# More unsplit tiles, a port in the planner's costs, and the first batch's global queries moved beside tiles 16 to 31

## The chip, the cores and the metric

The kernel runs on one core of a Trainium2 chip. The metric is the device time of one execution in microseconds (us). A core has five engines that run their own instruction streams and meet at semaphores: TensorE (PE in the profile, with its weight loads as PEld), VectorE (DVE), ScalarE (ACT), GpSimd (POOL) and SyncE (SP), which here only issues DMAs. TensorE writes to PSUM; the other data lies in SBUF.

## The reference

Attention with two kinds of queries feeds an MLP with a maximum in it. There are 8 batches, 8 heads, 512 local and 32 global positions and 64 dimensions a head.

```python
k_all = concat([k_g, k_l]); v_all = concat([v_g, v_l])
out_g = softmax(scale * q_g @ k_all.T) @ v_all            # 32 global queries see everything
s_ll  = where(|i - j| <= 32, scale * q_l @ k_l.T, -1e9)   # local queries: a band, and the globals
s_l   = concat([scale * q_l @ k_g.T, s_ll])
out_l = softmax(s_l) @ concat([v_g, v_l])
x = concat([out_g, out_l], axis=2).transpose(0, 2, 1, 3).reshape(8 * 544, 512)
h = max(max(x @ w1, x @ w2), x @ w3)                      # 512 -> 768
return h @ w_out                                          # 768 -> 512
```

## The kernel before

**Tiles.** Two heads make a pair, so there are 4 pairs a batch and 32 in all. A pair's 512 local queries are cut into 4 tiles of 128, so there are 128 tiles; tile number = 4 * pair + t. `SEQ` is the order in which they are taken: the 16 tiles of the first batch first, then 16, 17 and on. Per tile, `scores` makes the banded scores for both heads (PE into PSUM tile `S`, a reducing DVE instruction at L325, the exponential on ACT at L327, a scaling by `times`), a DMA brings them to a buffer `prob`, `trans` transposes them on PE into PSUM tile `T` (L345, L346) and copies them to `pt`, and `pv` multiplies with the values into PSUM tile `O` (L384 or L392). Scores are made three tiles ahead.

**Split and unsplit.** In most tiles every operand is split into a rounded number and a remainder (tiles `qs`, `kst`, `vs`, the second half of `pt`): a copy makes the first, a subtraction the second, and PE multiplies with both. In the first tiles the operands are used whole in plain float32: `NATK` names the tiles whose queries and keys are unsplit, `NAT` the number of tiles whose probabilities and values are (both 20). An unsplit `pv` needs one copy out of `O`; a split one needs a copy and three additions (L398, L400).

**Global queries.** `glob` (two steps) and `glob_soft` make the 32 global queries' softmax of one pair, which six small DMAs bring to `probg`; `transg` transposes a quarter of it for each tile on PE (L364), into an `S` tile, and copies it beside the tile's own probabilities, so that `pv` treats both at once. `S` tiles have two PSUM buffers, `T` and `O` one each. The first batch's tiles go without: its global queries are made at the end by `late`, a pair after the other: loads, `glob`, `glob_soft`, three transposes (L490), 12 small products (L500).

**The MLP.** `moe_local(b)` yields after every matmul, and `fill(n)` puts n of its matmuls at a place in the attention: 432 matmuls with 256 columns (L424) and 72 with 512 (L445) for the first batch, which are spread over tiles 8 to 31 of `SEQ`; 216 and 72 with 512 columns for each other batch b, beside the attention of batch b + 1. After the last tile come the last batch's MLP with the four `late` pairs among its matmuls, and `moe_glob` for all global queries.

**Weights.** The 24 weight pieces arrive as 8-byte floats. `convert` makes float32 of them with one ACT and four DVE instructions (L160 to L166), then a copy and a subtraction. That happens at tiles 0 to 23.

**Who does what.** `sub` (L97), `copy` (L103, L105) and `times` (L111, L113, L115) may run on several engines. `least` picks the one whose running total in `load` plus its cost is lowest; `spend` books fixed work, `settle` lets totals lag no more than 4.5 us behind the highest at each tile. The order on each engine is then set by the framework's scheduler from the program's order.

## Time and profile before

| what | value |
|---|---|
| time before, median of 3 (lowest, highest) | 860.33 us (859.11, 861.3) |
| the profiled execution: its own time, its span | 859.92 us, 858.0 us |
| PE, PEld busy | 95%, 80% of the span |
| DVE, POOL, ACT busy | 74%, 61%, 59% |
| mean granted TensorE clock | 0.99 |

The page gives for each engine its busy time and for each group of instructions how many there are, the mean time of one, and what ended the idle time before them. Matmuls overlap, so the mean of one (its latency) is longer than the step from one to the next; steps are read from the chain of waits, which gives a start, a length and a name for each piece of the work that ended last. Busy shares are means over stages with different limits, so the table by stretches of time is read first.

### The profile page before, as it was taken

The page shows a single profiled execution, that of the slowest core. Times are in us where ns is not written, and L with a number is a line of the kernel's source. Part 1 is how long each engine was busy: PE and PEld are TensorE (multiplying, and loading weights), DVE is VectorE, ACT ScalarE, POOL GpSimd, SP SyncE. Part 2 cuts the span into 40 slices and gives each one's busy share as a digit, 9 for nine tenths or more (in the row PEclk, how much of TensorE's full clock was granted, in tenths as well). Part 3 has the DMA queues.
Part 4 walks back from the last instruction along what each step waited for, and adds up shares of the span by engine and source line. Part 5 has one row for each costly group of instructions (what it writes and reads, how often), then busy time and mean ns, then how long its engine had stood idle before and what let it go on. Part 6 is the DMA issues. An engine that isn't in the chain of part 4 may idle for free.

```text
span 858.0 us, 16764 instructions
## 1 busy us (share of the span) xinstructions
PE 813.2 (95%) x4736; PEld 683.5 (80%) x4736; DVE 631.0 (74%) x2182; ACT 505.8 (59%) x1430; POOL 526.4 (61%) x695
## 2 busy tenths in 40 slices
PE   6877777999999999999999999999999999999997
PEld 5556667888888888888888888788888888777796
DVE  6999788978888887878787888787887876322111
ACT  6666566766675767676666666676667665212111
POOL 4779878766677667766776667666686656101211
PEclk9999799999999999999999999999999999999999
DMA  9843533353334333443325333433344332221000
GB/s 315 278 151 120 165 120 102 112 161 105 112 111 131 119 96 105 129 137 98 95 91 160 107 111 111 141 114 96 101 132 134 93 102 90 75 72 29 28 25 25
DMA packets 99580, 98.72 MB, mean 115 GB/s; under 512 B 21152, under 2 KB 87968, under 8 KB 99488
## 3 DMA queue, kind: packets, MB, share of 16 engines
q1 hardware_dynamic: 99344, 97.43, 36.5%
q8 instruction: 38, 0.62, 0.3%
q14 instruction: 54, 0.44, 0.2%
q10 hardware_dynamic: 144, 0.23, 0.1%
HBM read 60.39 MB, written 8.91 MB: 81 GB/s over the span
## 4 chain that ended last, share of the span: by engine, by line
PE 82%; DVE 5%; DMA 5%; POOL 4%; issue 2%; ACT 1%; SPq 0%; DVEq 0%; POOLq 0%; ACTq 0%
PE pm L424 47%; PE pm L445 16%; PE O L392 7%; PE S L322 5%; PE T L345 2%; DMA raw<-w_in 2%; PE T L346 2%; PE S L274 1%; POOL h L97 1%; DMA qn<-q_in 1%; POOL xs L97 1%; PE S L364 1%; POOL w L97 1%; POOL early L115 1%; DMA vraw<-v_in 1%
## 5 line engine op out<-in xcount | busy, mean ns | idle before, releaser
L424 PE MATMUL pm<-xs,w 128*128 128x512 f32 (+1 forms) x2160 | 501.5, 370 | 5.3 <-POOL w L97 3.8
L424 PEld LDWEIGHTS pm<-xs,w 128*128 128x128 f32 x2160 | 349.5, 191 | 56.2 <-POOL w L97 4.2
L445 PE MATMUL pm<-w,h 128*128 128x512 f32 x612 | 160.3, 399 | 1.8 <-POOL h L97 1.8
L97 POOL TENSOR_TENSOR qs<-qraw,qs 128x256 fp32r<-128x256 f32 x108 | 83.2, 770 | 75.6 <-issue 42.2
L97 POOL TENSOR_TENSOR h<-m,h 128x512 fp32r<-128x512 f32 (+1 forms) x60 | 72.3, 1205 | 87.8 <-ACT h L105 87.8
L445 PEld LDWEIGHTS pm<-w,h 128*128 128x128 f32 x612 | 107.2, 188 | 22.6 <-POOL h L97 3.7
L115 POOL TENSOR_SCALAR s<-s,z 128x224 f32<-128x224 f32 (+1 forms) x212 | 97.0, 467 | 42.8 <-ACT lox L105 18.5
L327 ACT ACTIVATE s<-s,nm 128x192 f32<-128x192 f32 (+1 forms) x224 | 103.3, 462 | 25.4 <-DVE nm L325 19.9
L433 DVE TENSOR_TENSOR m<-pm,m 128x512 f32<-128x512 f32 (+1 forms) x120 | 72.9, 607 | 49.4 <-PE pm L424 47.1
L97 DVE TENSOR_TENSOR pt<-T,pt 128x512 fp32r<-128x512 f32 x108 | 74.5, 690 | 38.8 <-ACT pt L105 36.4
L325 DVE CUSTOM_DVE_ANT_0 s<-S,mask 128x192 f32<-128x192 f32 (+1 forms) x224 | 74.6, 370 | 12.7 <-PE S L322 6.4
L97 POOL TENSOR_TENSOR vs<-vraw,vs 128x256 fp32r<-128x256 f32 x107 | 80.3, 751 | 4.9 <-ACT vs L105 4.0
L105 ACT CAST pt<-T 128x512 fp32r<-128x512 f32 x89 | 52.0, 584 | 46.9 <-PE T L346 46.8
L392 PE MATMUL O<-pt,vs 128*128 128x320 f32 (+1 forms) x432 | 77.8, 302 | 0.1
L392 PEld LDWEIGHTS O<-pt,vs 128*128 128x128 f32 x432 | 70.0, 189 | 9.3 <-DVE pt L97 0.3
L97 POOL TENSOR_TENSOR kst<-kraw,kst 64x576 fp32r<-64x576 f32 x48 | 70.6, 1471 | 5.6 <-DVE nm L325 1.5
L322 PEld LDWEIGHTS S<-kst,qs 128*128 128x128 f32 x432 | 64.4, 192 | 11.1 <-DVE nmg L278 3.2
L400 DVE TENSOR_TENSOR xr<-O,lox 64x160 f32<-64x160 f32 x216 | 67.9, 314 | 2.8
L105 ACT CAST qs<-qraw 128x256 fp32r<-128x256 f32 x90 | 36.6, 406 | 56.6 <-PE S L322 39.5
L322 PE MATMUL S<-kst,qs 128*128 128x192 f32 (+1 forms) x432 | 66.0, 275 | 1.2 <-DVE nmg L278 1.2
L398 DVE TENSOR_TENSOR lox<-O,lox 64x320 f32<-64x320 f32 x108 | 51.6, 478 | 13.4 <-ACT lox L105 7.2
L105 ACT CAST h<-m 128x512 fp32r<-128x512 f32 (+1 forms) x59 | 32.9, 558 | 40.6 <-DVE m L433 40.5
(118 smaller groups left out, 1196.4 us busy)
## 6 DMA issues: line engine op xcount, KB each, us to landing
vraw<-v_in SPq DMA_DIRECT2D x132, 128.0 KB, 2.3
qraw<-q_in SPq DMA_DIRECT2D x108, 128.0 KB, 2.2
prob<-s SPq DMA_DIRECT2D x56, 224.0 KB, 2.4
raw<-w_in SPq DMA_DIRECT2D x24, 512.0 KB, 4.8
prob<-s SPq DMA_DIRECT2D x56, 192.0 KB, 2.3
kraw<-k_in SPq DMA_DIRECT2D x27, 320.0 KB, 3.2
out_dram<-o SPq DMA_DIRECT2D x32, 256.0 KB, 2.3
qn<-q_in SPq DMA_DIRECT2D x21, 128.0 KB, 3.8
```

The costliest lines, as they stand in the source:

```text
L97: (dve if least(c) == "d" else pool).tensor_tensor(out=out, in0=a, in1=b, op=ALU.subtract)
L105: act.copy(out=out, in_=a)
L115: pool.tensor_scalar(out=out, in0=a, scalar1=col, scalar2=1.0, op0=ALU.mult, op1=ALU.mult)
L322: pe.matmul(ph[j][:, 0:n], lhsT=qs[sl][:, a, 128 * j:128 * j + 128], rhs=kst[p][:, j, c0:c0 + n], start=(a == 0), stop=(a == 1))
L325: dve.tensor_tensor_reduce(out=s[:, j, 0:n], in0=ph[j][:, 0:n], in1=mask[:, (1, 0, 1, 0)[t], 32 * (t == 0):32 * (t == 0) + n], scale=-0.12 ...
L327: act.activation(out=s[:, j, 0:n], in_=s[:, j, 0:n], func=AF.Exp, bias=nm[:, j:j + 1], scale=-1.0, accum_out=z[:, j:j + 1])
L392: pe.matmul(o[:, j, 0:320].rearrange("p (a q) -> p a q", a=2)[:, :, 0:n], lhsT=vs[sl][:, 2 * j + c].rearrange("p a d -> p (a d)"), rhs=pt[ ...
L398: dve.tensor_tensor(out=lo, in0=o[0:64, :, 160:320], in1=lo, op=ALU.add)
L400: dve.tensor_tensor(out=xr[p][64 * j:64 * j + 64, t], in0=o[0:64, j, 0:160], in1=lo[:, j], op=ALU.add)
L424: pe.matmul(ps[:, 0:n], lhsT=weight(3 * f + i, w)[:, 128 * k:128 * k + 128], rhs=xs[k][:, a, c0:c0 + n], start=(q == 0), stop=(q == 11))
L433: dve.tensor_tensor(out=m[:, 0:n], in0=ps[:, 0:n], in1=m[:, 0:n], op=ALU.max)
L445: pe.matmul(ps, lhsT=hh[f][:, a, 128 * t:128 * t + 128], rhs=weight(18 + f, w), start=(q == 0), stop=(q == 17))
```

## The change

1. `NATK` goes from 20 to 28 tiles and `NAT` from 20 to 26: queries and keys of tiles 20 to 27 and probabilities and values of tiles 20 to 25 are no longer split.
2. The first batch's global queries are made at tiles 16 to 31, a pair in four tiles, one step a tile after that tile's `pv`. A pair's keys and its four value tiles are loaded into one tile `side`, which takes the place of `early` (free after the first 16 tiles). The softmax is made in it; six windows of 128 columns are transposed by PE straight from it into one `S` tile, and one DVE multiplication with a 0/1 mask `cover` copies them out and clears what a window has too much. The six DMAs a pair through `probg` are gone. The end of the program holds no attention any more.
3. `transg` of a tile stands at the tile's own start, just ahead of the next tile's `trans`; it stood in the middle of the tile before.
[...]
5. The keys of pairs 5 and 6 are no longer split, so their `split_k` falls away.

```diff
-NATK = range(0, 20)
+NATK = range(0, 28)
...
-    load = {"a": 0.0, "d": 0.0, "p": 0.0}
+    load = {"a": 0.0, "d": 0.0, "p": 0.0, "x": 0.0}
+    shared = [True]
...
     def least(costs):
-        e = min(costs, key=lambda e: load[e] + costs[e])
-        load[e] += costs[e]
-        return e
+        if not shared[0]:
+            costs = {es[0]: ns for es, ns in costs.items()}
+        es = min(costs, key=lambda es: max(load[e] for e in es) + costs[es])
+        spend(es, costs[es])
+        return es[0]
...
     def sub(out, a, b, psum=False):
-        n = width(out)
-        c = {"d": n * 1.04 + (160 if psum else 110)}
+        n, k = width(out), 0 if shared[0] else 45
+        c = {"d" if psum else "dx": n * 1.04 + 75 + k + (40 if k and psum else 0)}
         if not psum:
-            c["p"] = n * 2.32 + 130
+            c["px"] = n * 2.32 + 80 + k
...
     def times(out, a, col):
-        n = width(out)
-        e = least({"d": n * 0.52 + 125, "a": n * 0.833 + 185, "p": n * 1.27 + 150})
+        n, k = width(out), 0 if shared[0] else 1
+        e = least({"dx": n * 0.52 + 60 + 65 * k, "a": n * 0.833 + 190, "px": n * 1.27 + 170 - 20 * k})
...
-    NAT = 20
+    NAT = 26
...
     def late(p):
-        load_k(p)
-        for t in range(4):
-            load_v(4 * p + t, p * 4 + t)
+        k, v = side[:, 0:640], side[:, 640:1664].rearrange("p (t x) -> p t x", t=4)
+        nc.sync.dma_start(out=k, in_=kin[p])
+        nc.sync.dma_start(out=v, in_=vin[4 * p:4 * p + 4].rearrange("t p x -> p t x"))
         yield
-        for i in range(2):
-            glob(p, i)
+        s, nm, z = side[0:64, 0:NG], small.tile([64, 2], F32, name="nmg"), small.tile([64, 2], F32, name="zg")
+        for i, (c0, n) in enumerate(SEG):
+            ps = psS.tile([128, 512], F32, name="S")
+            pe.matmul(ps[0:64, 0:n], lhsT=k[:, KW:KW + 2 * SG], rhs=k[:, c0:c0 + n], start=True, stop=True)
+            dve.tensor_tensor_reduce(out=s[:, 384 * i:384 * i + n], in0=ps[0:64, 0:n], ...)
         yield
-        glob_soft(p)
+        soft(s, nm, z)
         yield
-        gt = att.tile([128, 3, 128], F32, name="gt", tag="pt")
-        for i in range(3):
-            g = psS.tile([128, 512], F32, name="S")
-            pe.transpose(g.bitcast(F32R)[:, 0:128], probg[p % 2][:, i], identr)
-            copy(gt[:, i], g[:, 0:128], True)
-        yield
+        g = psS.tile([128, 512], F32, name="S")
+        for x, (t, c, c0) in enumerate(PARTS):
+            pe.transpose(g[:, 64 * x:64 * x + 64], side[0:64, c0:c0 + 128], one[0:64, 0:64])
+        gt = att.tile([128, 6, 64], F32, name="gt", tag="lox", bufs=1)
+        dve.tensor_tensor(out=gt, in0=g[:, 0:384]..., in1=cover.to_broadcast([128, 6, 64]), op=ALU.mult)
         o = psO.tile([128, 2, 512], F32, name="O")
...
         settle(4500)
+        shared[0] = i < 26
...
+        if i >= EARLY:
+            transg(sl)
         trans(tile_at(i + 1))
...
-            if i == 14:
-                split_k(5)
-                load_k(6)
         elif t == 3:
             split_k(p + 2)
+            if p == NP:
+                load_k(6)
             load_k(p + 3)
         fill(5 if first else 4)
         pv(sl)
+        if EARLY <= i < 32:
+            if i == EARLY:
+                side = const.tile([128, 2048], F32, name="side", tag="early")
+            if i % 4 == 0:
+                lates = late(i // 4 - 4)
+            next(lates)
...
         fill(3)
-        if i + 1 >= EARLY:
-            transg(tile_at(i + 1))
         fill(7)
...
     mm[0] = moe_local(B - 1)
-    for p in range(NP):
-        for _ in late(p):
-            fill(10)
     fill(400)
```

Three places show what it does to the engines' order. The first is POOL in the first 16 tiles; `early` is the probabilities' buffer there, `w_...<-spare` a weight's remainder, `xs` an MLP input's. Before:

```order
L115 TENSOR_SCALAR early<-early,z 128x224 x2
L97 TENSOR_TENSOR w_436<-spare,w_436 128x512
L97 TENSOR_TENSOR xs<-xr,xs 128x256
L115 TENSOR_SCALAR early<-early,z 128x224 x2
L97 TENSOR_TENSOR w_483<-spare,w_483 128x512
L115 TENSOR_SCALAR early<-early,z 128x192 x2
L97 TENSOR_TENSOR w_493<-spare,w_493 128x512
L97 TENSOR_TENSOR xs<-xr,xs 128x256
L97 TENSOR_TENSOR w_537<-spare,w_537 128x512
```

Of the change, from the same place (the third to the sixth weights' remainders on POOL):

```order
L125 TENSOR_SCALAR early<-early,z 128x224 x2
L103 TENSOR_TENSOR w_349<-spare,w_349 128x512
L103 TENSOR_TENSOR w_437<-spare,w_437 128x512
L103 TENSOR_TENSOR w_544<-spare,w_544 128x512
L103 TENSOR_TENSOR w_614<-spare,w_614 128x512
L103 TENSOR_TENSOR h_563<-m,h_563 128x256
```

Up to the first 160-column `pv`, POOL issues 9 scalings of `early` instead of 30, 7 weight remainders instead of 15, 3 remainders of `xs` instead of 7, and no remainder of `kst` instead of 2. DVE gets 8 more weight remainders and 4 of `xs`, ACT 18 scalings instead of 1.

The second place is PE in a tile of the later batches, with `S<-identr,probg` the global queries' transpose, `T` the tile's transpose and `pm` the MLP. Before:

```order
L392 MATMUL O<-pt,vs 128x320 x4
L424 MATMUL pm<-xs,w_493 128x512 x3
L364 MATMUL S<-identr,probg_96 128x128
L424 MATMUL pm<-xs,w_493 128x512 x7
L345 MATMUL T<-identr,prob_94 128x128
```

Of the change:

```order
L409 MATMUL O<-pt,vs 128x320 x4
L441 MATMUL pm<-xs,w_494 128x512 x10
L381 MATMUL S<-identr,probg_96 128x128
L362 MATMUL T<-identr,prob_94 128x128
L363 MATMUL T<-identr,prob_94 96x128
```

The global transpose now stands against the tile's own, behind ten MLP matmuls in a row.

The third place is PE in the last batch's MLP. Before, each of the four pairs stands there like this:

```order
L270 MATMUL S<-kn 64x384
L270 MATMUL S<-kn 64x160
L424 MATMUL pm<-xs,w_493 128x512 x12
L424 MATMUL pm<-xs,w_537 128x512 x12
L424 MATMUL pm<-xs,w_607 128x512 x5
L490 MATMUL S<-identr,probg_96 128x128 x2
L424 MATMUL pm<-xs,w_607 128x512 x2
L500 MATMUL O<-gt,vn 64x32 x2
```

Of the change, the first pair's last step, at tile 19 (its two scores, L504, stand at tile 17):

```order
L441 MATMUL pm<-xs,w_396 128x256 x10
L513 MATMUL S<-one,side 128x64 x6
L401 MATMUL O<-pt,vraw 64x160 x4
L441 MATMUL pm<-xs,w_396 128x256 x2
L441 MATMUL pm<-xs,w_437 128x256 x6
L362 MATMUL T<-identr,prob_94 128x128
L519 MATMUL O<-gt,side 64x32 x12
```

In the last batch's MLP the change has MLP matmuls alone.

More of the change, by code (lines that the diff above doesn't have):

```diff
@@ L77, in width, with spend @@
         return n
-    def spend(e, ns):
-        load[e] += ns
+    def spend(es, ns):
+        for e in es:
+            load[e] += ns
     def least(costs):
-        e = min(costs, key=lambda e: load[e] + costs[e])
-        load[e] += costs[e]
-        return e
+        if not shared[0]:
[3 more added lines that the diff above has]
+        return es[0]
     def settle(ns):
@@ L92, in sub @@
     def sub(out, a, b, psum=False):
-        n = width(out)
-        c = {"d": n * 1.04 + (160 if psum else 110)}
+        n, k = width(out), 0 if shared[0] else 45
+        c = {"d" if psum else "dx": n * 1.04 + 75 + k + (40 if k and psum else 0)}
         if not psum:
-            c["p"] = n * 2.32 + 130
+            c["px"] = n * 2.32 + 80 + k
         (dve if least(c) == "d" else pool).tensor_tensor(out=out, in0=a, in1=b, op=ALU.subtract)
     def copy(out, a, psum=False):
-        n = width(out)
-        c = {"d": n * (1.04 if psum else 0.52) + (160 if psum else 150), "a": n * 0.833 + (150 if psum else 190)}
+        n, k = width(out), 0 if shared[0] else 75
+        c = {"a": n * 0.833 + (80 if psum else 110) + k}
+        if psum:
+            c["d"] = n * 1.04 + 80 + k
+        else:
+            c["dx"] = n * 0.52 + 75 + k
         if least(c) == "d":
@@ L107, in times @@
     def times(out, a, col):
-        n = width(out)
-        e = least({"d": n * 0.52 + 125, "a": n * 0.833 + 185, "p": n * 1.27 + 150})
+        n, k = width(out), 0 if shared[0] else 1
+        e = least({"dx": n * 0.52 + 60 + 65 * k, "a": n * 0.833 + 190, "px": n * 1.27 + 170 - 20 * k})
         if e == "d":
@@ L118, in body @@
     make_identity(nc, one)
-    early = const.tile([128, 4, 2, 256], F32, name="early")
+    early = const.tile([128, 4, 2, 256], F32, name="early", tag="early")
     identr = const.tile([128, 128], F32R, name="identr")
@@ L127, in body @@
     qgz = const.tile([128, 2, 160], F32R, name="qgz")
+    cover = const.tile([128, 6, 1], F32, name="cover")
     def clear():
+        pool.memset(cover, 1.0)
+        for x, a, n in ((1, 0, 32), (2, 96, 32), (3, 0, 64), (4, 0, 32), (5, 64, 64)):
+            pool.memset(cover[a:a + n, x], 0.0)
         for t in (*probg, qgz):
@@ L166, in convert @@
         dve.scalar_tensor_tensor(out=c, in0=r[:, :, 0], scalar=29, in1=c, op0=ALU.logical_shift_right, op1=ALU.bitwise_or)
-        spend("d", 1900)
+        spend("dx", 1900)
         yield
@@ L285, in glob_soft, with soft @@
         s, nm, z = pg[p]
+        soft(s, nm, z)
+        for c0, n, i, h, d0 in GPUT:
+            nc.sync.dma_start(out=f32(probg[p % 2])[64 * h:64 * h + 64, i, d0:d0 + n], in_=s[:, c0:c0 + n])
+    def soft(s, nm, z):
         dve.tensor_tensor(out=nm[:, 0:1], in0=nm[:, 0:1], in1=nm[:, 1:2], op=ALU.min)
@@ L292, in glob_soft @@
         times(s, s, z[:, 0:1])
-        for c0, n, i, h, d0 in GPUT:
-            nc.sync.dma_start(out=f32(probg[p % 2])[64 * h:64 * h + 64, i, d0:d0 + n], in_=s[:, c0:c0 + n])
     def scores(sl):
@@ L484, in late @@
         yield
[L485 removed]
+        soft(s, nm, z)
         yield
[L487 to L492 removed]
+        g = psS.tile([128, 512], F32, name="S")
+        for x, (t, c, c0) in enumerate(PARTS):
+            pe.transpose(g[:, 64 * x:64 * x + 64], side[0:64, c0:c0 + 128], one[0:64, 0:64])
@@ L493, in late @@
+        gt = att.tile([128, 6, 64], F32, name="gt", tag="lox", bufs=1)
+        dve.tensor_tensor(out=gt, in0=g[:, 0:384].rearrange("p (x g) -> p x g", g=64), in1=cover.to_broadcast([128, 6, 64]), op=ALU.mult)
         o = psO.tile([128, 2, 512], F32, name="O")
-        todo = [(t, c) for t in range(4) for c in range(GCH[t][2])]
-        for x in todo:
-            t, c = x
-            i, h, _ = GCH[t]
+        for x, (t, c, _) in enumerate(PARTS):
             for j in range(2):
-                g0 = 64 * h + 64 * c + 32 * j
-                pe.matmul(o[64 * j:64 * j + 64, 0, 0:SG], lhsT=vraw[4 * p + t][:, 2 * j + c], rhs=gt[:, i, g0:g0 + SG],
-                          start=(x == todo[0]), stop=(x == todo[-1]))
+                pe.matmul(o[64 * j:64 * j + 64, 0, 0:SG], lhsT=v[:, t, 64 * (2 * j + c):64 * (2 * j + c) + 64],
+                          rhs=gt[:, x, SG * j:SG * j + SG], start=(x == 0), stop=(x == 5))
```

4 lines of the change are left out of this document (added).

## The prediction

> **What bounds the kernel now.** First the table of busy time in four stretches: tiles 0 to 15, tiles 16 to 31, tiles 32 to 127, and what follows the attention.
>
> ```profile
> core 0: us, PE busy (x) PEld busy (x) DVE busy (x) ACT busy (x) POOL busy (x), PEclk, DMA share, GB/s
> 0.00:92.00 92.00, 69.57 (x472) 55.45 (x473) 82.61 (x257) 58.19 (x162) 66.81 (x78) 0.97 0.63 208
> 92.00:187.00 95.00, 80.25 (x554) 72.22 (x553) 80.88 (x283) 62.88 (x183) 72.62 (x94) 0.94 0.44 136
> 187.00:738.60 551.60, 549.83 (x3052) 463.40 (x3051) 443.54 (x1580) 364.58 (x1038) 367.85 (x503) 1.00 0.37 113
> 738.60:858.00 119.40, 113.53 (x664) 92.43 (x662) 23.95 (x64) 20.19 (x47) 19.16 (x21) 1.00 0.13 38
> ```
>
> From 187 us on PE is the bound: 549.83 of 551.60 us. Before that it is not: DVE is busy 82.61 of 92 us, and between 92 and 187 us PE idles for 14.75 us while no other engine is full, so there it waits for chains through DVE and POOL. At the end, with DVE and POOL nearly idle, whatever stands on PE is paid in full.
>
> Second, the chain of waits, for that end:
>
> ```profile
> 738.57 2.27 PE pm L424 x10
> ...
> 797.32 5.46 PE pm L424 x23
> 802.78 16.32 PE pm L445 x72
> 819.10 25.91 PE pm L424 x216
> ```
>
> From 738.57 to 802.78 us runs layer 1 of the last batch, 216 matmuls with 512 columns, and among them the four `late` pairs. Layer 2, the same shape undisturbed, steps at 16.32 / 72 = 0.2267 us; the x23 piece at 0.237. The last row gives the step with 256 columns: 0.120 us.
>
> **The end.** `late` leaves it. Left are 216 x 0.2267 = 49.0 us of 64.21: 15.2 us gone (12.9 by the step 0.237). DVE's evictions there have room (23.95 us in 119.4), so PE's step decides. I take **-15**.
>
> **Tiles 16 to 31.** What `late` costs comes here. PE's own work in this stretch:
>
> ```profile
> L424 PE MATMUL pm<-xs,w 128*128 128x256 f32 x241 | 39.5, 301 | 3.6 <-POOL w L97 3.6
> L445 PE MATMUL pm<-w,h 128*128 128x512 f32 x72 | 19.0, 400 | 0.0
> ```
>
> At the steps above these take 241 x 0.120 + 72 x 0.2267 = 45.2 us. The attention's share comes from the steady batches, three of which lie between these two rows of the chain:
>
> ```profile
> 350.73 1.11 POOL xs L97
> ...
> 628.49 1.12 POOL xs L97
> ```
>
> A batch takes 277.76 / 3 = 92.6 us; less 288 x 0.2267 = 65.3 that is 27.3 us for 16 tiles. So PE needs 72.5 of the 95 us, and the rest, 22.5, is room. Into it go the four pairs. Some forms are new (transposes of 64 rows through `one`, the values from `side`); I price the pairs by what the old ones took, waits included: 15.2 us. That is the upper end, since part of it was waiting; nothing of it is the lower end only if all lay under other work, which a PE queue in order excludes. And plain float32 scores cost more than split ones (one tile's four rows of each):
>
> ```profile
> 73.86 0.92 PE L318 MATMUL S<-kn,qn 128*128 128x224 f32 x4
> ...
> 111.35 0.60 PE L322 MATMUL S<-kst,qs 128*128 128x224 f32 x4
> ```
>
> That is 0.32 x 8 tiles = 2.6 us. PE's floor becomes 72.5 + 15.2 + 2.6 = 90.3 us. The other engines lose work: six tiles lose these DVE additions and the remainder of `pt`, against four pairs with two reductions, a masked copy and five small steps.
>
> ```profile
> L398 DVE TENSOR_TENSOR lox<-O,lox 64x320 f32<-64x320 f32 x108 | 51.6, 478 | 13.4 <-ACT lox L105 7.2
> L400 DVE TENSOR_TENSOR xr<-O,lox 64x160 f32<-64x160 f32 x216 | 67.9, 314 | 2.8
> L97 DVE TENSOR_TENSOR pt<-T,pt 128x512 fp32r<-128x512 f32 x108 | 74.5, 690 | 38.8 <-ACT pt L105 36.4
> ```
>
> Away go 6 x (0.48 + 2 x 0.31 + 0.69) = 10.7 us; an estimate for the pairs is 4 x 2 = 8 us, by the rows of 0.48 and 0.69 for the like sizes. DVE falls a little below its 80.88, POOL issues 39 instructions where it issued 79, and ACT, which takes over 20 scalings, has 32 us free. So PE becomes the bound here. It will still wait now and then: at tiles 17, 21, 25 and 29 two late scores and one `glob` ask for the two `S` buffers in a row, each behind a DVE reduction, which I put at 0.5 us a pair on top of the old waits already in the 15.2. That makes about 91 of 95: **-4**, with ends at -10 (only half of the 15.2 was work) and +4 (more waits at `S` and `O`).
>
> **Tiles 0 to 15.** The planner moves work from POOL to DVE and ACT. Whether this pays hangs on how far the two disturb each other. Groups, then pieces of the chain:
>
> ```profile
> L165 DVE SCALAR_TENSOR_TENSOR spare<-raw,spare 128x512 int32<-128x512 int32 x18 | 20.2, 1123 | 0.0
> L166 DVE SCALAR_TENSOR_TENSOR spare<-raw,spare 128x512 int32<-128x512 int32 x18 | 16.8, 936 | 0.0
> L97 POOL TENSOR_TENSOR w<-spare,w 128x512 fp32r<-128x512 f32 x18 | 25.3, 1407 | 5.5 <-ACT w L105 4.1 <-DVE w L103 1.2
> L115 POOL TENSOR_SCALAR early<-early,z 128x224 f32<-128x224 f32 x16 | 10.7, 677 | 11.6 <-DVE identr L121 8.0 <-DVE z L331 1.5 <-DVE z L330 1.4
> ```
>
> ```profile
> 80.73 1.42 POOL kst L97
> 82.25 0.97 POOL s L115
> ...
> 104.82 0.60 DVE wct L166
> ...
> 106.55 0.41 DVE wct L162
> ...
> 127.28 1.46 DVE wct L162
> ```
>
> The same DVE instruction takes 0.41 us once and 1.46 at another time, and L166 takes 0.60 at its quickest against a mean of 0.94: DVE is slowed beside POOL. The excess over 0.60 of the two groups is 18 x (0.52 + 0.34) = 15.5 us. POOL loses 21 scalings (0.68), 8 weight remainders (1.41), 4 of `xs` (half of that) and 2 of `kst` (1.42): 31 of its 66.81 us. I let the excess fall in proportion, by 7 us. DVE gains 8 weight remainders at 0.69 (nearest row: `pt<-T,pt`, same width) and 4 of half the width: 6.9. So DVE breaks even, and the gain is a chain: at 80.73 us the first split tiles' scaling (`s`, 82.25) queued on POOL behind remainders of `kst`, which are gone. I take 1.42 + 0.97 and something for the shorter POOL queue: **-4**. Ends: +7 (no relief for DVE) and -12.
>
> **Tiles 32 to 127.** The global transpose joins the tile's own. What a separate one costs stands in the timeline:
>
> ```profile
> 406.62 0.56 ACT L105 CAST pt<-T 128x512 fp32r<-128x512 f32 x1
> ...
> 407.22 0.69 DVE L97 TENSOR_TENSOR pt<-T,pt 128x512 fp32r<-128x512 f32 x1
> ...
> 408.46 0.67 PEld L392 LDWEIGHTS O<-pt,vs 128*128 128x128 f32 x4
> ...
> 409.20 0.85 PE L424 MATMUL pm<-xs,w 128*128 128x512 f32 x3
> ...
> 409.89 0.22 PE L364 MATMUL S<-identr,probg 128*128 128x128 f32 x1
> ...
> 409.95 1.81 PE L424 MATMUL pm<-xs,w 128*128 128x512 f32 x7
> ...
> 411.60 0.22 PE L345 MATMUL T<-identr,prob 128*128 128x128 f32 x1
> ...
> 411.85 0.46 PE L424 MATMUL pm<-xs,w 128*128 128x512 f32 x1
> ```
>
> From 409.20 to 411.60 us lie ten MLP matmuls (2.27 us) and one transpose: it costs 0.13 us. The four of `T` take 0.25, or 0.06 each. So leaving and entering the MLP costs some 0.07 us by itself, which the merged one saves: 96 x 0.07 = 6.7 us at most, nothing at least if the excess belongs to the products just before. I take **-5**.
>
> **Sum.** Against the profiled execution's 859.92 us: 859.9 - 15 - 4 - 4 - 5 = 831.9, so 832. Its time is 0.4 us under the median, which changes nothing.
>
> **Rivals.** (1) *The idle time of tiles 16 to 31 stays.* If its chains (scores to DVE to DMA to transpose) set the pace, the late work and the dearer scores come on top: +17.8 - 3 for what the pairs' waits overlap, so 832 + 4 + 14.8 = 851. For it: before, PE idled with no engine full. Against: half of POOL's instructions and its slowing of DVE go.
>
> (2) *POOL and DVE exclude each other, and that was the bound.* Then each us taken from POOL is a us for DVE: 31 off, 6.9 on, so tiles 0 to 15 lose 24 us, but ACT (58.19 plus 17 scalings at no more than POOL's 0.68) and PE (69.57) stop it near 74 us: -18 in place of -4, so 818. The 1.46 against 0.41 speaks for it, the means of only 0.94 to 1.12 and DVE's 82.61 busy us in 92 against it. [...]
>
> (3) *Slower: `pv` waits for the global transpose's copies.* They used to have ten MLP matmuls more. Now ACT's copy and DVE's remainder must be through between the transposes (about 406.1, ahead of the 406.62 row) and `pv`'s weights at 408.46. With one ACT copy and one DVE remainder of a quarter the size of the two rows shown, they end near 407.3: 1.2 us to spare. If queues on ACT and DVE ran later than that in most tiles, by 0.4 us on average, 112 tiles would lose 45 us: 877. It decides from 0.25 us a tile on. Against: ACT and DVE stand idle for about a fifth of this stretch or more.
>
> (4) *The end does not shrink*, since layer 1 there waited for something else: 832 + 15 = 847. The chain names only PE there, but for the first pair's loads.
>
> **Chances.** Forecast 0.70; idle stays 0.13; port 0.11; slower 0.03; end stays 0.03. The time predicted is the forecast's, 832. Its own ends add up to 859.9 - 15.2 - 10 - 12 - 6.7 = 816 and 859.9 - 12.9 + 4 + 7 = 858; all four terms do not go one way, so about half of each side: 822 to 845. Taking in the port's 818 and most of rival 1 gives 817 to 849. A change of over 0.3% is what a measurement of this kernel can tell (its three runs lie within 0.25%). Faster: all but rival 3 and the outermost corner of the rest, 0.96; within 0.3%: 0.01; slower: 0.03.
>
> **What would show it.** The profile after should have: MLP matmuls without a break from the end of the attention to the end, over some 107 us; PE busy for more than 95% between tiles 16 and 32, in about 91 us; the first tile with global queries some 4 us earlier, POOL's busy time before it near half, and L165's and L166's means (L180, L181 there) nearer to 0.8 us; 91.8 us a batch in place of 92.6. The prediction is wrong if PE idles over 8 us between tiles 16 and 32, if `pv` waits for `pt<-S` in the steady batches, or if DVE's busy time before tile 16 grows.

## The result and the profile after

The changed kernel takes **829.76 us** (median of 4 runs, 828.83 to 830.49), the kernel before, run beside it, 860.63 us (859.11 to 861.3). The ratio is 0.9643 (95% interval 0.9625 to 0.9661). Predicted were 832 us and 817 to 849. The profiled execution took 830.49 us, its span is 828.7.

The table of busy time by stretches, for the kernel after, with the borders at the same places of the program as in the prediction's table: the first transpose of the global queries (tile 16), the first layer-1 matmul of the second batch's and of the last batch's MLP.

```profile
core 0: us, PE busy (x) PEld busy (x) DVE busy (x) ACT busy (x) POOL busy (x), PEclk, DMA share, GB/s
0.00:84.80 84.80, 68.88 (x472) 55.90 (x473) 74.18 (x266) 65.27 (x184) 24.93 (x40) 0.95 0.75 249
84.80:176.50 91.70, 89.32 (x715) 76.21 (x713) 77.61 (x297) 63.12 (x189) 50.72 (x61) 0.99 0.53 159
176.50:724.50 548.00, 545.20 (x3051) 465.27 (x3051) 446.52 (x1600) 366.74 (x1015) 367.32 (x506) 1.00 0.37 110
724.50:828.70 104.20, 99.55 (x541) 86.46 (x539) 16.52 (x30) 15.07 (x30) 16.34 (x17) 0.99 0.06 18
```

| stretch | before, us | after, us | difference | predicted |
|---|---|---|---|---|
| tiles 0 to 15 | 92.0 | 84.8 | -7.2 | -4 |
| tiles 16 to 31 | 95.0 | 91.7 | -3.3 | -4 |
| tiles 32 to 127 | 551.6 | 548.0 | -3.6 | -5 |
| from the last batch's MLP on | 119.4 | 104.2 | -15.2 | -15 |

The end is as simple as the prediction had it. The chain of waits after, from 724 us on (start, length, what): layer 1 of the last batch in one piece of 216 matmuls, 48.96 us.

```profile
724.65 48.96 PE pm L441 x216
773.61 16.34 PE pm L462 x72
789.95 25.91 PE pm L441 x216
```

Between tiles 16 and 31 PE idles 2.4 us where it idled 14.75. Before tile 16 POOL works 24.93 us where it worked 66.81, and DVE, which converts the weights there, is faster. Its groups of instructions in that stretch, after (behind the count: busy us, mean ns | us idle before; L180, L181, L176 and L177 are L165, L166, L161 and L162 of before):

```profile
L180 DVE SCALAR_TENSOR_TENSOR spare<-raw,spare 128x512 int32<-128x512 int32 x18 | 16.8, 931 | 0.0
L181 DVE SCALAR_TENSOR_TENSOR spare<-raw,spare 128x512 int32<-128x512 int32 x17 | 12.0, 703 | 0.0
L176 DVE TENSOR_SCALAR spare<-spare 128x512 f32<-128x512 f32 x18 | 10.6, 595 | 0.0
L177 DVE TENSOR_SCALAR spare<-spare 128x512 int32<-128x512 int32 x18 | 7.6, 426 | 0.0
```

They add up to 47.0 us (one record of L181 is missing). Before, they add up to 58.9: L165 and L166, as in the prediction, 20.2 and 16.8, and

```profile
L162 DVE TENSOR_SCALAR spare<-spare 128x512 int32<-128x512 int32 x18 | 11.2, 628 | 0.0
L161 DVE TENSOR_SCALAR spare<-spare 128x512 f32<-128x512 f32 x18 | 10.7, 599 | 0.2 <-ACT spare L160 0.2
```

The stretches between tile 0 and 31 are where several parts of the change meet, and where the total alone says least. Most experiments go there.

### The profile page after: what moved, and what is told of

Read it like the earlier page. It is cut to its first block, busy times and chain, and to the rows that moved or that the text cites. A ratio compares the mean times of both kernels' runs of the same rounds, so it can differ in the third digit from the quotient of the medians.

```text
span 828.7 us, 16580 instructions
## 1 busy us (share of the span) xinstructions
PE 803.0 (97%) x4772; PEld 683.8 (83%) x4772; DVE 614.8 (74%) x2192; ACT 510.2 (62%) x1416; POOL 459.3 (55%) x623
## 4 chain that ended last, share of the span: by engine, by line
PE 80%; DVE 5%; DMA 4%; issue 3%; ACT 3%; POOL 3%; SPq 1%; POOLq 0%; ACTq 0%; DVEq 0%
PE pm L441 45%; PE pm L462 16%; PE O L409 6%; PE S L339 5%; PE T L362 2%; PE T L363 2%; DMA prob<-s 2%; PE S L289 1%; PE S L335 1%; POOL h L103 1%; PE O L401 1%; DMA vraw<-v_in 1%; ACT s L344 1%; PE S L381 1%; DMA raw<-w_in 1%
## 5 line engine op out<-in xcount | busy, mean ns | idle before, releaser
L441 PE MATMUL pm<-xs,w 128*128 128x512 f32 (+1 forms) x2160 | 487.3, 366 | 1.3 <-ACT m L115 0.9
L441 PEld LDWEIGHTS pm<-xs,w 128*128 128x128 f32 x2160 | 354.3, 190 | 52.7 <-issue 4.2
L103 POOL TENSOR_TENSOR qs<-qraw,qs 128x256 fp32r<-128x256 f32 x100 | 76.7, 767 | 70.4 <-issue 34.8
L344 ACT ACTIVATE s<-s,nm 128x192 f32<-128x192 f32 (+1 forms) x224 | 103.3, 462 | 19.6 <-DVE nm L342 14.1
L125 POOL TENSOR_SCALAR s<-s,z 128x224 f32<-128x224 f32 (+1 forms) x192 | 83.9, 444 | 36.1 <-ACT lox L115 20.4
L342 DVE CUSTOM_DVE_ANT_0 s<-S,mask 128x192 f32<-128x192 f32 (+1 forms) x224 | 74.5, 369 | 15.2 <-PE S L339 7.0
L103 POOL TENSOR_TENSOR vs<-vraw,vs 128x256 fp32r<-128x256 f32 x102 | 75.6, 741 | 12.6 <-ACT vs L115 9.3
L409 PE MATMUL O<-pt,vs 128*128 128x320 f32 (+1 forms) x408 | 72.9, 300 | 1.4 <-DVE pt L103 1.4
L339 PEld LDWEIGHTS S<-kst,qs 128*128 128x128 f32 x400 | 59.5, 190 | 8.7 <-DVE nmg L293 0.2
L103 POOL TENSOR_TENSOR kst<-kraw,kst 64x576 fp32r<-64x576 f32 x44 | 63.9, 1453 | 4.3 <-DMA prob<-s 1.0
L115 ACT CAST pt<-T 128x512 fp32r<-128x512 f32 x102 | 60.3, 591 | 9.5 <-PE T L363 7.1
L339 PE MATMUL S<-kst,qs 128*128 128x192 f32 (+1 forms) x400 | 59.5, 270 | 0.0
L347 DVE TENSOR_SCALAR z<-z 128x1 f32<-128x1 f32 x256 | 37.5, 147 | 27.1 <-ACT s L344 17.9
```

The source lines that it names most:

```text
L103: (dve if least(c) == "d" else pool).tensor_tensor(out=out, in0=a, in1=b, op=ALU.subtract)
L115: act.copy(out=out, in_=a)
L125: pool.tensor_scalar(out=out, in0=a, scalar1=col, scalar2=1.0, op0=ALU.mult, op1=ALU.mult)
L339: pe.matmul(ph[j][:, 0:n], lhsT=qs[sl][:, a, 128 * j:128 * j + 128], rhs=kst[p][:, j, c0:c0 + n], start=(a == 0), stop=(a == 1))
L342: dve.tensor_tensor_reduce(out=s[:, j, 0:n], in0=ph[j][:, 0:n], in1=mask[:, (1, 0, 1, 0)[t], 32 * (t == 0):32 * (t == 0) + n], scale=-0.12 ...
L344: act.activation(out=s[:, j, 0:n], in_=s[:, j, 0:n], func=AF.Exp, bias=nm[:, j:j + 1], scale=-1.0, accum_out=z[:, j:j + 1])
```

## The experiments

Each kernel is the changed kernel with the edit shown. Times are medians of 4 runs; the kernel before, run with each set, took 859.7 to 859.9 us, so times of different sets can be compared. The three stretches are those of each kernel's own profiled execution; the first one lies between 82.4 and 86.5 us in kernels that differ from the changed kernel only later, so it scatters by about 2 us either way, and less than that is not read from it.

What the title and the table call the planner's port is a fourth total in `load`, `x`: up to tile 25, DVE's and POOL's work without PSUM is booked on it as well as on the engine itself, and the costs are changed; from tile 26 on the costs are within 10 ns of the old ones and `x` plays no part in a choice. It stands for the author's assumption that the two engines get in each other's way; the runs show only by how much DVE is slower beside POOL.

| kernel | time, us | ratio to before (95%) | tiles 0-15 | tiles 16-31 | tiles 32-127 |
|---|---|---|---|---|---|
| the changed kernel | 829.8 | 0.9643 (0.9625 to 0.9661) | 84.8 | 91.7 | 548.0 |
| late pairs at the end | 838.2 | 0.9753 (0.9738 to 0.9767) | 86.4 | 84.8 | 547.6 |
| 20 unsplit tiles | 841.2 | 0.9782 (0.9765 to 0.9798) | 84.2 | 104.3 | 547.2 |
| both | 845.7 | 0.9847 (0.9824 to 0.9871) | 82.0 | 95.8 | 547.4 |
| 24 unsplit tiles | 834.2 | 0.9705 (0.9685 to 0.9724) | 83.5 | 95.7 | 547.6 |
| 32 unsplit tiles | 829.0 | 0.9648 (0.9615 to 0.9681) | 86.3 | 92.8 | 547.8 |
| planner without the port | 842.6 | 0.9804 (0.9788 to 0.9821) | 89.1 | 98.5 | 547.8 |
| port to tile 15 only | 834.8 | 0.9714 (0.9696 to 0.9731) | 82.4 | 97.4 | 547.6 |
| nothing on POOL to tile 15 | 835.4 | 0.9718 (0.9698 to 0.9738) | 87.9 | 94.8 | 546.9 |
| global transpose back | 835.1 | 0.9711 (0.9697 to 0.9726) | 84.5 | 93.2 | 551.3 |
| scores at the transposes | 835.3 | 0.9712 (0.9673 to 0.9751) | 82.5 | 95.0 | 552.6 |
| late pairs a tile later | 834.8 | 0.9710 (0.9688 to 0.9732) | 84.2 | 95.5 | 549.2 |
| the last two together | 837.0 | 0.9742 (0.9713 to 0.9770) | 82.4 | 95.7 | 551.9 |

### What makes room for the late pairs

First, the late pairs at the end again, among the last batch's MLP:

```diff
-        if EARLY <= i < 32:
-            ...
-            next(lates)
...
     mm[0] = moe_local(B - 1)
+    side = const.tile([128, 2048], F32, name="side", tag="early")
+    for p in range(NP):
+        for _ in late(p):
+            fill(10)
```

> The four late pairs, in their new form, stand among the last batch's MLP again, one after the other with ten MLP matmuls between their steps; all else is as in the changed kernel. My theory (the end pays them in full because nothing else runs there; at tiles 16 to 31 they cost nearly as much, since PE is full there): the end grows by 12 to 16 us, the stretch of tiles 16 to 31 falls from 91.7 us by 6 to 10 us, PE is no longer full in it, and the time is 834 to 838 us. Rival (the late work fits into the idle time that stage had, so the move was worth the whole 15 us): the stretch of tiles 16 to 31 stays within 2 us of 91.7, and the time is 842 to 847 us.

838.2 us, 8.4 more than the changed kernel. The rows of its tiles 16 to 31 and of its end, in the columns of the table above:

```profile
86.40:171.20 84.80, 78.70 (x574) 68.82 (x572) 71.01 (x260) 57.88 (x174) 45.80 (x55) 0.99 0.42 128
718.80:835.80 117.00, 111.99 (x677) 92.38 (x675) 24.12 (x63) 18.66 (x41) 19.13 (x21) 1.00 0.12 38
```

The end grows by 12.8 us and tiles 16 to 31 shrink by 6.9, as the theory had it (the time is 0.2 us over its range). The rival, that the pairs fit into idle time there, is excluded. Its chain shows what a pair costs PE, in its new form:

```profile
721.22 1.06 PE S L504 x4
...
727.08 0.52 PE S L513 x6
...
728.72 0.82 PE O L519 x24
```

1.06 + 0.52 + 0.82 = 2.4 us a pair, 9.6 for four (PE's busy time in tiles 16 to 31 gives 89.32 - 78.70 = 10.6). Of this 6.9 us lengthen the stretch and some 3 lie in idle time.

Second, 20 unsplit tiles as before the change, with the late pairs where the change put them:

```diff
-NATK = range(0, 28)
+NATK = range(0, 20)
-    NAT = 26
+    NAT = 20
...
+            if i == 14:
+                split_k(5)
+                load_k(6)
...
-            if p == NP:
-                load_k(6)
```

> Both numbers of unsplit tiles are 20 again, and the keys of pairs 5 and 6 are split where they were before; the late pairs, the port and the transposes are as in the changed kernel. My theory (the split tiles' remainders load DVE, POOL and ACT between tiles 12 and 25, and before tile 16 the remainders of keys stand in front of the first split tiles' scalings): the first global transpose comes 1 to 3 us later than 84.8 us, the stretch of tiles 16 to 31 stays or grows by up to 3 us, and the time is 831 to 835 us. Rival (plain scores cost PE 0.32 us a tile more, and PE is the bound there, so undoing it gains 8 x 0.32 = 2.6 us): 827 to 828 us.

841.2 us, 11.4 more, all of it in tiles 16 to 31; neither of the two cases. Its row there, and what PE waited for (us in total, times, longest):

```profile
84.20:188.50 104.30, 91.94 (x693) 77.05 (x691) 87.25 (x326) 75.77 (x223) 60.87 (x75) 0.97 0.46 142
```

```profile
PE O L409 <- DVE pt L103: 2.7, 4, 1.4
PE S L513 <- POOL side L125: 2.5, 1, 2.5
```

PE idles 12.4 us again, in many waits, of which these are the two largest groups, while DVE (84%) and ACT (73%) have fuller queues and no engine is full. PE's busy time does not fall although the plain scores are gone (91.94 against 89.32 us; some 2 us of the difference are the lower clock, 0.97 against 0.99), so their price of 0.32 us a tile is not to be seen here. And tiles 0 to 15 take 84.2 us: of the two remainders of keys that stood in POOL's queue before tile 16, one is back there (1.49 us, at 70.8 us) and the other is on DVE. They cost nothing, but no scaling of `s` stands behind them on POOL, so the queue that the prediction priced is not made again here.

Third, both edits together:

> The late pairs at the end and 20 unsplit tiles, both together: what is left of the change is the planner's port, the new place of the global transpose and the late pairs' new form. Each alone gave 838.2 and 841.2 us, 8.4 and 11.4 us over the changed kernel. Theory (the unsplit tiles are what makes room for the late pairs beside tiles 16 to 31; without the late pairs the split tiles fit): the second step costs less than alone, at most 5 us, so 839 to 843 us, with the stretch of tiles 16 to 31 at 85 to 90 us. Rival (the two are independent): the costs add, 848 to 851 us, stretch 96 to 98 us.

845.7 us, between the two cases; tiles 16 to 31, at 95.8 us, lie next to the rival's 96.

```profile
82.00:177.80 95.80, 80.50 (x556) 71.00 (x555) 82.70 (x296) 71.28 (x207) 56.50 (x72) 0.96 0.41 124
```

By the times, the unsplit tiles are worth 11.4 us with the late pairs beside them and 7.5 without (845.7 - 838.2). But of these 4 us most lie before tile 16 (82.0 and 86.4 us), in the scatter; in tiles 16 to 31 themselves the unsplit tiles are worth 12.6 us with the pairs (104.3 - 91.7) and 11.0 without (95.8 - 84.8). So nearly all of their gain has nothing to do with the pairs, and that the two help each other is not shown. The row shows more: without unsplit tiles and without the pairs, PE idles 15.3 us in 95.8, as it idled 14.75 in 95.0 before the change, although the planner's port and the new place of the transpose are in this kernel.

Then the number itself. 24 in both places (the keys of pair 6 loaded at tile 14):

```diff
-NATK = range(0, 28)
+NATK = range(0, 24)
-    NAT = 26
+    NAT = 24
...
+            if i == 14:
+                load_k(6)
...
-            if p == NP:
-                load_k(6)
```

> 24 unsplit tiles in both numbers instead of 28 and 26 (20 gave 841.2 us); the rest as in the changed kernel. Theory (each split tile between 20 and 27 adds waits on the way from PSUM, in proportion): half of the 11.4 us, 834 to 837 us. Rival (plain scores cost PE 0.32 us a tile and PE is full, a few split tiles fit): 827 to 830 us. The stretch of tiles 16 to 31 also holds pauses of PE after which the granted clock can fall to a half, 1.7 us each, which spreads either figure by 2 us.

and 32 in both:

```diff
-NATK = range(0, 28)
+NATK = range(0, 32)
-    NAT = 26
+    NAT = 32
```

> All tiles up to 31 unsplit, in both numbers, the rest as in the changed kernel. Theory (at 28 and 26 PE is already full in this stretch, so further relief of the other engines gives nothing and the plain scores of four more tiles cost 4 x 0.32 us): 830 to 833 us. Rival (the waits that are left at the split tiles 26 to 31 still count): 824 to 828 us.

With 20, 24, 28 (26 for the values) and 32 the times are 841.2, 834.2, 829.8 and 829.0 us; 24 lies in the range of its theory. The gain fades as PE fills up: with 32, DVE is busy 67 of the stretch's 92.8 us and PE 91.83. The runs with 32 lie from 827.0 to 832.9 us, so it can't be told from the changed kernel, nor the two cases from each other.

### The planner's port

Without `x`, at the costs of tile 26 and later from the first tile on:

```diff
-    shared = [True]
+    shared = [False]
...
-        shared[0] = i < 26
+        shared[0] = False
```

> [...] My theory (the gain before tile 16 comes from taking work off POOL, which slows DVE): the first global queries' transpose comes 3 to 6 us later than the 84.8 us of the changed kernel, the two long conversions on DVE are back near 1.1 and 0.95 us, and the time is 833 to 837 us. Rival (the gain came from the keys' remainders that no longer stand in POOL's queue, so the planner's port does nothing): the mark stays within 1 us of 84.8, the time is 829 to 831 us. Rival by the prediction's second case (POOL and DVE exclude each other all the time): the mark goes back to 92 us or later, time 837 us and more.

842.6 us, 12.9 more: 4.3 us in tiles 0 to 15 and 6.8 in tiles 16 to 31. POOL is back at 62.83 us before tile 16, the conversions at 1025 and 976 ns (their rows up to 84.8 us):

```profile
0.00:89.10 89.10, 68.66 (x473) 53.79 (x473) 78.12 (x256) 56.18 (x158) 62.83 (x80) 1.00 0.63 214
89.10:187.60 98.50, 89.78 (x712) 75.58 (x713) 75.92 (x286) 57.45 (x174) 64.27 (x85) 1.00 0.55 169
```

```profile
L180 DVE SCALAR_TENSOR_TENSOR spare<-raw,spare 128x512 int32<-128x512 int32 x17 | 17.4, 1025 | 0.0
L181 DVE SCALAR_TENSOR_TENSOR spare<-raw,spare 128x512 int32<-128x512 int32 x16 | 15.6, 976 | 0.0
```

So the theory holds for the first stretch, and the exclusive case, which asked for 92 us or later, does not; the time lies over the theory's 837 us, since the port's larger effect, in tiles 16 to 31, was not in it. What PE waited for before tile 16 says more than the means of DVE. Before the change, without the port, and after it, two rows of each:

```profile
PE T L345 <- POOL early L115: 10.1, 10, 1.6
PE T L345 <- DMA prob<-s: 4.9, 2, 4.7
```

```profile
PE T L362 <- POOL early L125: 9.8, 11, 1.5
PE T L362 <- DMA prob<-s: 2.4, 1, 2.4
```

```profile
PE T L362 <- ACT early L123: 2.4, 5, 1.2
PE T L362 <- POOL early L125: 0.8, 1, 0.8
```

The port takes POOL's scalings out of PE's way, 9.8 us of waits becoming 0.8; some waits for ACT and DVE come in their place, so 4.3 us are left of it. The other row shows the prediction's own chain: without the port POOL has the scalings of `s` still, but the remainders of keys ahead of them are gone, the scalings end at 82.5 us instead of 85.1, and the longest wait for the transfer behind them falls from 4.7 to 2.4 us.

Is the effect in tiles 16 to 31 work left over from before, or the shares in tiles 16 to 25 themselves? The port to tile 15 only:

```diff
-        shared[0] = i < 26
+        shared[0] = i < 16
```

> The planner's port holds until tile 15 only instead of 25; the rest as in the changed kernel (without the port at all it was 842.6 us, of which 4.3 us arose before the first global transpose and 6.8 us in tiles 16 to 31). Theory (POOL's and DVE's shares in tiles 16 to 25 matter by themselves): the first global transpose stays at 84 to 86 us, the stretch of tiles 16 to 31 is at 96 to 99 us, the time 834 to 838 us. Rival (tiles 16 to 31 only suffered from the work left over from before): the stretch is at 91 to 93 us, the time 829 to 831 us.

834.8 us, 5.0 more. The first stretch keeps its gain (82.4 us), the second is at 97.4, with POOL at 66.47 us where the changed kernel has 50.72. The shares in tiles 16 to 25 count by themselves.

```profile
82.40:179.80 97.40, 90.06 (x714) 75.87 (x714) 77.77 (x295) 59.45 (x176) 66.47 (x83) 1.00 0.50 152
```

Next, nothing of remainders and scalings on POOL until tile 15, which goes further the way the port went:

```diff
+    barred = [True]
...
     def sub(out, a, b, psum=False):
...
-        if not psum:
+        if not psum and not barred[0]:
             c["px"] = n * 2.32 + 80 + k
...
     def times(out, a, col):
-        e = least({"dx": ..., "a": ..., "px": n * 1.27 + 170 - 20 * k})
+        c = {"dx": ..., "a": ...}
+        if not barred[0]:
+            c["px"] = n * 1.27 + 170 - 20 * k
+        e = least(c)
...
+        barred[0] = i < 16
```

> Until tile 15 neither remainders nor scalings may go to POOL; DVE and ACT do what POOL did there (25 us of POOL's time). All else as in the changed kernel. Theory A (POOL slows DVE only in part, and its own late answers were what counted; those are gone already): DVE gains some 11 us of work and loses the rest of the excess of its long conversions, 18 x (0.33 + 0.10) = 7.8 us; ACT and DVE are fuller, the first global transpose comes within 3 us of 84.8, the time is 827 to 834 us. Theory B, the prediction's second case (POOL and DVE exclude each other, so each us taken off POOL is one for DVE): 25 us off, 11 on, the mark falls to 75 to 78 us, where ACT and PE stop it, and the time is 820 to 823 us.

835.4 us, and the first stretch takes 87.9 us, not 75 to 78: theory B is out. Theory A is near, but both figures lie just outside it (3.1 us over 84.8 where 3 were allowed, and a time 1.4 us over its 834). The same groups of DVE (their lines are 4 higher here), and the row:

```profile
L184 DVE SCALAR_TENSOR_TENSOR spare<-raw,spare 128x512 int32<-128x512 int32 x17 | 11.6, 683 | 0.0
L185 DVE SCALAR_TENSOR_TENSOR spare<-raw,spare 128x512 int32<-128x512 int32 x17 | 11.6, 683 | 0.0
L180 DVE TENSOR_SCALAR spare<-spare 128x512 f32<-128x512 f32 x18 | 7.3, 413 | 0.0
L181 DVE TENSOR_SCALAR spare<-spare 128x512 int32<-128x512 int32 x17 | 7.1, 418 | 0.0
```

```profile
0.00:87.90 87.90, 70.72 (x476) 57.85 (x477) 74.88 (x287) 68.91 (x193) 2.17 (x15) 0.92 0.75 248
```

With POOL out of the way the four take 683 + 683 + 413 + 418 = 2197 ns a weight piece. Beside POOL's 24.93 us they take 2655, beside 66.81 us 3286: 18 pieces lose 8.2 and 19.6 us, about 0.3 us for each us that POOL works. DVE's busy time, 74.88 us, ends where it was, since it got POOL's work. That the stretch became longer by 3 us with no engine fuller than 85% is little more than the scatter; PE's granted clock is lower there (0.92 against 0.95), and its waits for ACT's scalings are 3.7 us instead of 2.4. Which of these counts is not settled. As much again is lost in tiles 16 to 31 (94.8 us), which the edit does not touch directly.

### The place of the transpose, and breaks in the MLP

```diff
-        if i >= EARLY:
+        if EARLY <= i < 32:
             transg(sl)
...
         fill(3)
+        if i + 1 >= 32:
+            transg(tile_at(i + 1))
         fill(7)
```

> From tile 32 on the global queries' transpose stands in the middle of the tile before again, with seven MLP matmuls between it and the tile's own transpose; until tile 31 it stands where the change put it. My theory (each break of the row of MLP matmuls costs PE 0.035 to 0.07 us by itself): 96 tiles x 0.035 to 0.07 = 3.4 to 6.7 us more, 833 to 836.5 us, at 92.4 us a batch instead of 91.8. Rival (the place of the transpose costs nothing, and the gain of the steady batches is from elsewhere): 829 to 830.5 us.

Tiles 32 to 127 take 551.3 us, against 548.0 after and 551.6 before: 3.3 us, or 0.034 us a tile, the lower end of what was expected. The time is 5.3 us more. Where the rest is from shows in tiles 16 to 31, where the edit changes nothing, but the stretch is 1.5 us longer. Both kernels pause there at the same place, waiting for the same remainder on DVE; here PE's timeline after, and the five us behind the pause:

```profile
145.49 0.82 PE L409 MATMUL O<-pt,vs 128*128 128x320 f32 x4 [1.37 <-DVE pt L103]
```

```profile
145.50:150.50 5.00, 5.00 (x59) 4.57 (x59) 4.41 (x18) 3.23 (x10) 2.59 (x5) 1.00 0.73 204
```

and with the transpose back:

```profile
145.13 0.82 PE L409 MATMUL O<-pt,vs 128*128 128x320 f32 x4 [1.35 <-DVE pt L103]
```

```profile
145.20:150.20 5.00, 5.00 (x31) 4.74 (x32) 3.55 (x17) 2.28 (x9) 1.87 (x4) 0.66 0.73 216
```

The granted clock (third figure from the right) is 1.00 after the one pause and 0.66 after the other: 5 x 0.34 = 1.7 us of PE's full speed lost. This is taken up below.

If a break in the MLP costs 0.034 us, one less should gain as much. Scores right behind the transposes, from tile 32 on:

```diff
-        fill(6 if first else 4)
+        if first:
+            fill(6)
         next_scores(i + 3)
...
-        fill(5 if first else 4)
+        fill(5 if first else 8)
```

> From tile 32 on the next scores stand right behind the tile's transposes, and the four MLP matmuls that stood between them join the four behind the scores: one break of the row of MLP matmuls less a tile, all else as in the changed kernel. My theory (each break costs PE 0.035 to 0.07 us, nothing else depends on it there): 96 x 0.035 to 0.07 = 3.4 to 6.7 us off, 823 to 826.5 us, 90.3 to 90.8 us a batch instead of 91.3. Rival (scores so early wait for the S buffer that the global transpose has just taken, until ACT and DVE have copied it): PE idles 0.3 us a tile or more, the time is 840 us or more. Rival (a break between transposes and scores is needed anyway): 829 to 831 us.

835.3 us, 5.6 more, with runs from 831.4 to 837.7; tiles 32 to 127 take 552.6 us. The forecast of the time falls, and no rival's time is met either; the first rival's wait is there, but in 3 of 96 tiles only. What PE waited for from tile 32 on:

```profile
PE S L339 <- DVE nmg L293: 5.4, 3, 2.0
```

Three waits of 1.6 to 2.0 us, for the `S` buffer that `glob` holds until DVE's reduction. At 526.8 us DVE is late since it splits keys (timeline of DVE; the reduction is L293):

```profile
522.84 1.62 DVE L113 CAST kst<-kraw 64x576 fp32r<-64x576 f32 x1
524.49 1.74 DVE L103 TENSOR_TENSOR kst<-kraw,kst 64x576 fp32r<-64x576 f32 x1
...
527.96 0.55 DVE L293 CUSTOM_DVE_ANT_0 sg<-S,sg 64x384 f32<-64x384 f32 x1
```

PE pauses 1.81 us, and then the clock falls, as it does behind two of the three waits:

```profile
528.00:530.00 2.00, 1.42 (x6) 1.33 (x7) 1.58 (x5) 0.31 (x1) 1.82 (x4) 0.69 0.17 53
530.00:532.00 2.00, 2.00 (x6) 1.54 (x5) 1.02 (x8) 1.08 (x5) 1.48 (x3) 0.50 0.67 219
```

The four MLP matmuls between transposes and scores were no mere break: they covered `S`. The price of a break itself is not refuted. Less 5.4 us of waits and 2 x 1.7 us of clock, tiles 32 to 127 would take 543.8 us, 4.2 under the changed kernel, or 0.044 us a tile: an estimate, but in the forecast's range.

### Two attempts at a better version

PE's pause at 81.5 to 82.7 us after stands in the chain behind a transfer of probabilities that took 4.86 us from 77.76 us on, beside the first loads for the late pairs. So each step of the late pairs one tile later:

```diff
-        if EARLY <= i < 32:
-            if i == EARLY:
+        if EARLY < i < 33:
+            if i == EARLY + 1:
...
-            if i % 4 == 0:
+            if i % 4 == 1:
```

> Each step of the late pairs stands one tile later (tiles 17 to 32 instead of 16 to 31), so that the first load of keys and values for them (two large transfers) does not stand beside the first transfers of the global queries' probabilities. Theory (the transfer of probabilities that took 4.86 us at 77.8 us of the changed kernel's trace was slowed by those loads, and PE waited for it): the first global transpose comes at 82 to 83.5 us, the time is 826 to 828.5 us. Rival (the transfer was slow for another reason, or PE only waits elsewhere then): 829 to 831 us.

834.8 us, neither of the two cases: the first stretch is 0.6 us shorter, within the scatter, and tiles 16 to 31 are 3.8 us longer, perhaps since the pairs now reach further into the split tiles; no run isolates that. And with the scores' edit:

> The scores right behind the transposes from tile 32 on, and the late pairs one tile later, together: if both theories hold and add, 820 to 825 us; if only the first does, 823 to 827 us; if neither, 829 to 831 us.

837.0 us, 7.2 more: worse than either alone, less than their sum. None of these kernels beats the changed kernel by more than can be measured.

## Why the prediction was right, and where not

The time was right, 832 against 829.8 us, with the sum of the terms at -28 and -29.3 in the traces. Two of the four terms came for the reasons given. The other two, tiles 0 to 15 and 16 to 31, had steps that failed, and that the whole still fits is in part luck: errors of either sign cancelled.

**The end, -15.** Right in place and size: -15.2 us, layer 1 in 48.96 us where 49.0 were worked out. Rival (4) is out.

**Tiles 16 to 31, -4.** -3.3 us, and PE became the bound as forecast, busy 97% of the stretch. But the terms of its floor, 72.5 + 15.2 + 2.6 = 90.3, were each off. The pairs, in their new form, cost PE 9.6 to 10.6 us, not 15.2. Without the pairs PE is busy 78.7 us, not 72.5 + 2.6. These errors cancelled, which is luck. More important is what the step took for granted, that the 14.75 us of idle time would be filled. It took "DVE falls a little" as the part of the unsplit tiles; the unsplit tiles, and with them in place the port in tiles 16 to 25, are what removed the idle time. With 20 unsplit tiles the stretch is 104.3 us with 12.4 idle, without the port 98.5 with 8.7, and with 20 unsplit tiles and no pairs 95.8 with 15.3. Rival (1), chance 0.13, describes the first two of these well, though at 841 to 843 us, not 851: so the rival was right on the mechanism, and the forecast was right that its condition falls away, but not on what makes it fall.

**What the step did not read.** The prediction quoted a granted clock of 0.94 for this stretch and made nothing of it. In 95 us that is up to 5.7 us of PE's full speed; after, at 0.99, 0.9 us. The difference is larger than the stretch's whole gain. Behind three pauses of 3.56, 3.01 and 2.07 us the kernel before ran at 0.66 for 5 us each, here the first and the last:

```profile
100.40:105.40 5.00, 5.00 (x32) 4.33 (x33) 3.13 (x12) 2.78 (x10) 3.46 (x5) 0.66 0.29 77
143.50:148.50 5.00, 4.98 (x26) 4.80 (x27) 3.85 (x15) 3.90 (x12) 3.46 (x3) 0.66 0.46 135
```

So idle time of PE cost more there than its length, and filling it gained more. Not all idle time does: without the port PE idled 8.7 us in this stretch at a granted clock of 1.00, with one pause of 2.4 us among it. The last section shows what can be read of the difference.

**Tiles 0 to 15, -4.** -7.2 us, within the ends given. Of the step, the larger part is borne out and the rest failed. The chain of `kst` ahead of a scaling, 1.42 + 0.97 = 2.4 us, shows in the kernel without the port: the wait behind it is 2.3 us shorter and the stretch 2.9 (by itself hardly above the scatter). What failed is "something for the shorter POOL queue", the remaining 1.6 us of the -4: it measured 4.3, because PE had waited 10.1 us for POOL's scalings of `early` in ten places, and no term priced these waits. DVE did not break even either: its four groups lost 11.4 us by their means (7 assumed, for two of them), and its busy time fell by 8.4 us. The 7 also came from a misreading. The 0.60 us for L166 is the piece of it that the chain shows, while that instruction took 0.68, so the excess of the two groups was nearer to 12.7 us than to 15.5.

**Rival (2), POOL and DVE exclude each other** ("port" among the chances). Out: with POOL all but idle until tile 15 (2.17 us busy) nothing was gained, 87.9 us against 84.8, and DVE's conversions lost 0.3 us per us of POOL, not 1. That POOL slows DVE, the runs show: the first conversion (L165, L180, L184) took 1123 ns beside 66.81 us of POOL's work, 931 beside 24.93 and 683 beside 2.17. A whole us for each us of POOL, on which the 818 rests that the range takes in, they do not show; a sum that takes it so would have missed by 12 us. Why it is a third no run here tells.

**Tiles 32 to 127, -5.** The mechanism was right and the size off: the price of leaving and entering the MLP was read as 0.07 us from one tile, at most, and taken as 0.05; the stretches give 0.034 to 0.038, so -3.3 to -3.6 us. Rival (3) did not come. All that PE waited for from 176 to 724 us after, and `pt` is not among it:

```profile
PE pm L462 <- POOL h L103: 2.1, 4, 0.5
PE T L362 <- DMA prob<-s: 0.5, 2, 0.3
```

**What would show it.** As said: the MLP without a break to the end, PE over 95% in 91.7 us, 91.8 us a batch, L180 and L181 at 0.93 and 0.70 us, DVE's busy time before tile 16 not grown. POOL fell to 37% of its time before, below the "half".

**The sum of the parts.** Undoing one part each gives 8.4 (late pairs), 11.4 (unsplit), 12.9 (port) and 5.3 us (transpose), together 38, where the whole change brings 30.9. They are not independent. Undoing the port costs 6.8 us in tiles 16 to 31, yet the kernel that has the port and the new place of the transpose, but neither pairs there nor more unsplit tiles, takes 95.8 us for them, where 95.0 were taken before the change. What the new place of the transpose is worth in tiles 16 to 31, and what the pairs' new form is worth by itself, no run isolates.

## What to carry to other kernels

A stretch where PE idles while no engine is full is not room to be filled by counting PE's work: what empties the queues around it (fewer operations a tile between PSUM and the next matmul, shares moved off POOL, where the remainder of a weight took 1.36 us after the change against 0.69 on DVE) has to come with the work that fills it, and here brought more than the move itself. Read the granted clock of each stretch and price a pause by what follows it: here 1.7 us more behind some, nothing behind others. And before a few matmuls between two attention steps are called a break and closed up, see which buffer they give time to come free.
